# A two-layer MoE kernel behind memory attention: the second matrix of layer two by seven block products

## The chip, the cores and the metric

The kernel runs on one core of one Trainium2 chip. The metric is the device time of one execution in microseconds. TensorE multiplies matrices and writes PSUM; VectorE and ScalarE do the elementwise work; SyncE (SP) issues nearly all DMAs. GpSimd does almost nothing here.

## The reference

Four batches of 576 tokens go through attention over 32 memory slots a head; its output, as 2304 rows of 512, goes through two MoE layers, each of two matrices with an activation between. All inputs are 8-byte floats that the kernel itself decodes to 4-byte ones.

```
h = x @ w_in                      # 2304 x 512 by 512 x 2048
g = np.maximum(0.01 * h, h)       # layer one
return g @ w_out                  # 2304 x 2048 by 2048 x 512

h = x @ w_in                      # layer two, same sizes
sp = np.where(h > 20.0, h, np.log1p(np.exp(np.minimum(h, 20.0))))
g = h * np.tanh(sp)               # Mish
return (g @ w_out).astype(np.float32)
```

## The kernel before

**Precision.** Every operand of the large matmuls is split into a high part (rounded to float32r) and a low part (the rest), and a product is made of three passes: high by high, high by low, low by high. `hi_lo` (line 308) makes the two parts: a copy on ScalarE or VectorE and a difference on VectorE.

**Layer one** (`stage1`, line 888) works on 128 items, one for a batch, a half of its tokens (288) and 128 of the 2048 inner columns. An item has 6 matmuls of 288 columns on line 899 and 12 on line 932; ScalarE and VectorE make the activation's high and low part between them.

**Layer two** works on super-tiles of 768 tokens (three of them) and units of 256 inner columns (eight a super-tile, 24 units in all). `unit` (line 1243) makes the first matrix by Strassen's scheme in Winograd's form: the 2 x 2 blocks of activations and weights are combined into seven products instead of eight, each of 6 matmuls of 384 columns (line 1262). Its sums of results lie in PSUM (banks `h0`, `h1`) and in SBUF; `keep` (line 1292) copies a running sum out on ScalarE before the next product is added to it, `plus` (line 1295) adds on VectorE, and `mish` (line 1275) applies the activation twice, once into the high part and once in full, from which VectorE takes the low part.

The second matrix, `second` (line 1324), is a plain one: a unit has four blocks (two of inner columns, two of tokens), each with three token tiles by three passes, 36 matmuls of 512 columns a unit (line 1336). They accumulate over the eight units of a super-tile in six PSUM banks; then the six are copied out and written, one DMA or more for each (line 1396). Its weights are split once, in `split_w_out` (line 1143), and stay in SBUF for all three super-tiles.

**Weights of layer two** are loaded, decoded and put to DRAM while layer one runs (the loop at line 851, 16 pairs, paced by `W2` and `W2S`). The combined parts of the first matrix are made in the first eight units (`split_w`, line 1080), saved to DRAM, and loaded back in later units.

**Order.** Nothing is written in its final order by hand. Every piece of work is a task with engines, a planned duration, a priority in units of items, the tasks it depends on and the buffers it takes. `Order.run` (line 94) plays the tasks through once and writes each engine's instructions in the order in which it places them. The engines then run their queues in that order, each waiting at its head. SP's queue has loads, saves and outputs in one line.

```
            {"ACT": act(n, ps), "DVE": dve(n) if ps else dve2(n)}, prio, lambda e: copy(e, hi(), src()), deps, take, use,
            lambda e: nc.vector.tensor_tensor(out=lo(), in0=src(), in1=hi().bitcast(F32), op=ALU.subtract),
                    out=ac[t].t, lhsT=(lb if x else hb).t[:, t * P:(t + 1) * P], rhs=wu[0].t[:, wi, :],
```

## Time and profile before

| what | value |
|---|---|
| median of 3 runs | 789.77 us (789.52 to 789.93) |
| profiled execution | 786.6 us |
| its span, first to last instruction | 784.8 us |
| TensorE busy | 767.2 us, 98% |
| VectorE busy | 449.1 us, 57% |
| ScalarE busy | 366.7 us, 47% |
| DMA | 133.27 MB, mean 170 GB/s |
| mean granted clock of TensorE | 0.995 |

Layer one lies roughly between 41 and 405 us, layer two between 393 and 777. Sums and comparisons are made against the profiled execution, since durations come from it; the median of the runs is 3.2 us above it. Busy time of TensorE is modelled at the end of a matmul and counts overlaps, so the distance from one start to the next is the measure of what a matmul costs.

### The profile page before, as it was taken

What the parts mean: (1) busy time and instruction counts of PE and PEld (TensorE: products, weight loads), DVE (VectorE), ACT (ScalarE), POOL (GpSimd) and SP (SyncE); (2) the same over time, 40 slices, a digit from 0 to 9 for tenths busy, and PEclk for the clock granted to TensorE, in tenths of its full rate; (3) what the DMA queues carried; (4) which work ended last, traced back from release to release, by engine and by line L of the source; (5) the groups of instructions that cost most, each with busy time, mean ns of one, the idle gap of its engine ahead of it and who ended that gap; (6) DMA issues with size and microseconds to landing.
All of it is one profiled execution on the core that took longest, in us unless ns stands there. A gap on an engine that the chain in (4) does not pass through costs nothing.

```text
span 784.8 us, 13670 instructions
## 1 busy us (share of the span) xinstructions
PE 767.2 (98%) x5328; PEld 694.7 (89%) x5328; DVE 449.1 (57%) x945; ACT 366.7 (47%) x829; POOL 0.7 (0%) x6
## 2 busy tenths in 40 slices
PE   7999999999999999999999999999999999999996
PEld 5798899998889989999998898888988898889884
DVE  3899868969666875674765566452223272122212
ACT  2576548655454664543554343334332344233322
POOL 0000000000000000000000000000000000000000
PEclk9999999999999999999999999999999999999998
DMA  9995496927978567531744444335432346334303
GB/s 221 266 335 150 133 262 190 299 70 228 300 225 262 165 215 268 162 109 54 280 177 162 174 175 161 121 120 175 134 121 94 122 134 188 108 115 136 98 1 80
DMA packets 57728, 133.27 MB, mean 170 GB/s; under 512 B 5184, under 2 KB 31808, under 8 KB 57664
## 3 DMA queue, kind: packets, MB, share of 16 engines
q1 hardware_dynamic: 57504, 132.14, 54.2%
q8 instruction: 42, 0.69, 0.4%
q10 hardware_dynamic: 160, 0.26, 0.2%
q14 instruction: 22, 0.18, 0.1%
HBM read 100.40 MB, written 31.98 MB: 169 GB/s over the span
## 4 chain that ended last, share of the span: by engine, by line
PE 87%; DMA 5%; DVE 4%; ACT 2%; issue 1%; SPq 0%; ACTq 0%; DVEq 0%
PE h_t L1262 22%; PE acc_t L932 22%; PE acc_t L1336 17%; PE h_t L899 11%; PE misc_t L1336 9%; DMA raw_t<-in_moe_w_in_dram 2%; DMA raw_t<-in_moe_w_out_dram 2%; PE misc_t L738 2%; PE acc_t L819 2%; PE misc_t L533 1%; PE misc_t L621 1%; DVE wo_t L317 1%; PE misc_t L652 1%; DMA phi_t<-in_phi_dram 1%; DVE lo_t L920 0%
## 5 line engine op out<-in xcount | busy, mean ns | idle before, releaser
L932 PE MATMUL acc_t<-hi_t,wo_t 128*128 128x288 f32 x1024 | 162.2, 299 | 0.9 <-ACT hi_t L913 0.3
L932 PEld LDWEIGHTS acc_t<-hi_t,wo_t 128*128 128x128 f32 x1024 | 142.6, 188 | 10.0 <-issue 6.6
L899 PE MATMUL h_t<-at_t,vw_t 128*128 128x288 f32 x768 | 123.8, 297 | 1.6 <-ACT e_t L913 1.5
L899 PEld LDWEIGHTS h_t<-at_t,vw_t 128*128 128x128 f32 x768 | 108.5, 188 | 3.7 <-ACT e_t L913 3.4
L913 ACT ACTIVATE hi_t<-h_t 128x288 fp32r<-128x288 f32 x128 | 52.6, 411 | 102.3 <-PE acc_t L932 90.0
L1297 DVE TENSOR_TENSOR e_t<-e_t,h_t 128x384 f32<-128x384 f32 x48 | 26.6, 554 | 119.0 <-ACT e_t L301 97.1
L932 PE MATMUL acc_t<-lo_t,wo_t 128*128 128x288 f32 x512 | 90.9, 299 | 0.4 <-DVE lo_t L920 0.4
L1262 PE MATMUL h_t<-xt_t,vw_t 128*128 128x384 f32 x432 | 87.4, 337 | 0.0
L920 DVE TENSOR_TENSOR lo_t<-e_t,hi_t 128x288 fp32r<-128x288 f32 x128 | 57.6, 453 | 46.8 <-ACT e_t L913 23.5
L1262 PEld LDWEIGHTS h_t<-xt_t,vw_t 128*128 128x128 f32 x432 | 77.3, 188 | 6.3
L1262 PE MATMUL h_t<-xt_t,wo_t 128*128 128x384 f32 x384 | 82.3, 335 | 0.0
L932 PEld LDWEIGHTS acc_t<-lo_t,wo_t 128*128 128x128 f32 x512 | 74.5, 188 | 8.0 <-issue 6.5
L1336 PE MATMUL acc_t<-wo_t,hi_t 128*128 128x512 f32 x288 | 79.1, 394 | 0.0
L1262 PEld LDWEIGHTS h_t<-xt_t,wo_t 128*128 128x128 f32 x384 | 68.8, 188 | 4.5
L301 ACT ACTIVATE e_t<-h_t 128x384 f32<-128x384 f32 x48 | 23.5, 490 | 98.1 <-PE h_t L1262 98.1
L1336 PEld LDWEIGHTS acc_t<-wo_t,hi_t 128*128 128x128 f32 x288 | 53.5, 188 | 9.7
L913 ACT ACTIVATE e_t<-h_t 128x288 f32<-128x288 f32 x128 | 52.1, 408 | 0.0
L1279 ACT ACTIVATE hi_t<-e_t 128x384 fp32r<-128x384 f32 x48 | 25.2, 526 | 55.9 <-DVE e_t L1297 53.6
L1287 DVE TENSOR_TENSOR lo_t<-e_t,hi_t 128x384 fp32r<-128x384 f32 x48 | 26.8, 558 | 40.0 <-ACT e_t L1282 39.8
L1287 DVE TENSOR_TENSOR lo_t<-x_t,hi_t 128x384 fp32r<-128x384 f32 x48 | 26.7, 557 | 33.5 <-ACT x_t L1282 33.5
L1336 PE MATMUL acc_t<-wo_t,lo_t 128*128 128x512 f32 x144 | 45.3, 394 | 0.0
L365 ACT ACTIVATE raw_t<-raw_t 128x512 f32<-128x512 f32 x46 | 31.5, 685 | 21.3 <-DMA raw_t<-in_moe_w_in_dram 17.1
(187 smaller groups left out, 1031.1 us busy)
## 6 DMA issues: line engine op xcount, KB each, us to landing
vw_t<-wsum SPq DMA_DIRECT2D x32, 512.0 KB, 3.5
raw_t<-in_moe_w_out_dram SPq DMA_DIRECT2D x24, 512.0 KB, 5.8
win_t<-wscr SPq DMA_DIRECT2D x24, 512.0 KB, 4.3
raw_t<-in_moe_w_in_dram SPq DMA_DIRECT2D x22, 512.0 KB, 5.5
wsum<-vw_t SPq DMA_DIRECT2D x16, 512.0 KB, 3.1
wo_t<-wsum SPq DMA_DIRECT2D x16, 512.0 KB, 3.4
kv_t<-in_k_dram SPq DMA_DIRECT2D x8, 576.0 KB, 10.2
kv_t<-in_v_dram SPq DMA_DIRECT2D x8, 576.0 KB, 11.5
```

The lines of the kernel that those rows point to most:

```text
L301: nc.scalar.activation(out=o, in_=i, func=AF.Copy)
L365: nc.scalar.activation(out=hf(), in_=hf(), func=AF.Copy, scale=2.0 ** -112)
L738: nc.tensor.matmul(out=pss[g].t[M * h:M * (h + 1), :], lhsT=vT[b, g][0].t[rows, h // 2, :], rhs=wbs[g].t[rows, h // 2, :], start=True, sto ...
L899: nc.tensor.matmul(out=h.t, lhsT=us[g][0].t[:, wi, j0:j0 + P], rhs=ats[g][0].t[:, ai, cols], start=(n == 0), stop=(n == 3 * NG - 1),)
L913: nc.scalar.activation(out=o, in_=h.t, func=AF.Prelu, alpha=0.01)
L920: lambda e: nc.vector.tensor_tensor(out=lb.make(), in0=eb.t, in1=hb.t.bitcast(F32), op=ALU.subtract),
L932: nc.tensor.matmul(out=ac[kk].t, lhsT=wu[0].t[:, wi, kk * P:(kk + 1) * P], rhs=(hb if src == 0 else lb).t, start=(first and (wi, src) == ( ...
L1262: nc.tensor.matmul(out=h.t, lhsT=w[:, wi, c0:c0 + P], rhs=xp[b, xi].ap()[:, j], start=(first and j == 0 and k3 == 0), stop=(j == 1 and k3 ...
L1279: {"ACT": act(NB2, ps)}, prio, lambda e: nc.scalar.activation(out=hb.make(), in_=src(), func=AF.Mish), deps, [hb], use
L1287: lambda e: nc.vector.tensor_tensor(out=lb.make(), in0=dst(), in1=hb.t.bitcast(F32), op=ALU.subtract),
L1297: {"DVE": dve(NB2)}, prio, lambda e: nc.vector.tensor_tensor(out=x(), in0=x(), in1=h.t, op=ALU.add), deps, (), [h, *use]
L1336: nc.tensor.matmul(out=ac[t].t, lhsT=(lb if x else hb).t[:, t * P:(t + 1) * P], rhs=wu[0].t[:, wi, :], start=(first and (wi, x) == (0, 0)) ...
```

## The change

The second matrix of layer two is also made by seven block products, over groups ("chunks") of four units. `second` and `split_w_out` go; a function `chunk` comes, called after every fourth unit.

- A unit now leaves its four result blocks, after the activation, in SBUF (24 places of 128 x 384, in slots that held layer one's weights, reused as chunks finish).
- `chunk` forms four sums of blocks a unit on VectorE, in place where it can, and for each of seven products and four units a high part (ScalarE or VectorE) and a low part (VectorE). Each product of a unit is three token tiles by three passes, 9 matmuls of 256 columns.
- A product accumulates over its four units in three PSUM banks of one of two sets ("ways"); the second product of a way is added onto the first. After a product its three tiles are copied or added into output rows in SBUF. After the second chunk of a super-tile the rows are written out, in halves of 256 columns.
- The seven combined weight parts of a pair of units are made during layer one, in high and low parts, and saved to DRAM (`t_scr`). `chunk` loads one part, 256 KB, for every product of a unit, into a ring of eight places.
- The loop that prepares the weights is spread further (`W2S` from 2.9 to 3.8) and takes more buffers, among them the tile of k and v of the attention part, widened to 128 partitions.
- Units 1 and 3 put their sums in the banks `acc0` and `acc1`, which the second matrix does not use yet.

```diff
-    A2=30, S2=2.6, V1=2.4, V2=14, W2=56.0, W2S=2.9, O='phi0 phi1 w0 q0 kv0 w1 kv1 w2 q1 w3', HF1=-8.0, HFS=1.0,
+    A2=30, S2=2.6, V1=2.4, V2=14, W2=56.0, W2S=3.8, O='phi0 phi1 w0 q0 kv0 w1 kv1 w2 q1 w3', HF1=-8.0, HFS=1.0,
...
+    DW=280e3, DQ=1.3, DP=1.5, L4=0.5, L4P=1.6, L4S=0.8, L4T=5.0, MA=6, MV="......rvvrrvvrvr",
...
+    kv_again = tags["kv"].new([P, 3, 1024])
+    opened = add({"SP": 0.0}, K["W2"], lambda e: kv_again.make(), (), [kv_again])
...
+    views = [View(j) for j in range(3)]
+    more = Ring(raw.slots + rawm.slots[3:])
+    w2_scr, t_scr = {}, {}
+    OS = ("B11", "B21", "B22", "T1", "T3", "T2", "T4")
     for n in range(NM):
 
         kind, u = "io"[n % 2], n // 2
         p = K['W2'] + K['W2S'] * n
-        bs = [load_raw(p + 2 * j - 6, kind, 2 * u + j) for j in range(2)]
-        wd = raw.new([P, 2, 512])
+        r0, r1, r2 = more.next(3) if n < K["MA"] else views if K["MV"][n] == "v" else raw.slots
+        bs = [load_raw(p + 2 * j - 6, kind, 2 * u + j, 0, r) for j, r in enumerate((r0, r1))]
+        wd = r2.new([P, 2, 512])
...
+        def fsum(e, wd=wd, sb=sb):
+            sb.make()
+            nc.vector.tensor_tensor(
+                out=sb.t[:, 0:2], in0=wd.t[:, :, 256:512], in1=wd.t[:, 0].rearrange("p (a f) -> p a f", a=2), op=ALU.subtract
+            )
+            nc.vector.tensor_tensor(out=sb.t[:, 2], in0=qd(wd, 1, 1), in1=sb.t[:, 0], op=ALU.subtract)
+            nc.vector.tensor_tensor(out=sb.t[:, 3], in0=qd(wd, 1, 0), in1=sb.t[:, 2], op=ALU.subtract)
...
+        def fhi(e, wd=wd, st=st):
+            st.make()
+            copy(e, st.t[:, 0], qd(wd, 0, 0))
+            copy(e, st.t[:, 1:3].rearrange("p a f -> p (a f)"), wd.t[:, 1])
...
+        def flo(e, wd=wd, st=st):
+            for i, x in ((0, qd(wd, 0, 0)), (1, wd.t[:, 1])):
+                y = st.t[:, 0] if i == 0 else st.t[:, 1:3].rearrange("p a f -> p (a f)")
+                nc.vector.tensor_tensor(out=x.bitcast(F32R), in0=x, in1=y.bitcast(F32), op=ALU.subtract)
...
+        def save1(e, u=u, st=st):
+            t_scr[u][0] = dram.tile([P, 7, 2, 256], F32, name=f"tscr{u}")
+            nc.sync.dma_start(out=t_scr[u][0][:, 0:3, 0], in_=st.t[:, 0:3].bitcast(F32))
+
+        def save2(e, u=u, wd=wd):
+            nc.sync.dma_start(out=t_scr[u][0][:, 0, 1], in_=qd(wd, 0, 0))
+            nc.sync.dma_start(out=t_scr[u][0][:, 1:3, 1], in_=wd.t[:, 1].rearrange("p (a f) -> p a f", a=2))
...
+    g_places(2)
     places(1)
-    w_out_place.extend(place([P, 2, 512]) for _ in range(NM - 2))
+    g_places(6)
+    for _ in range(4):
+        b = place([P, 2, 512])[1]
+        T_place.extend(Part(b, lambda t, j=j: t[:, j].rearrange("p (a f) -> p a f", a=2)) for j in range(2))
+    g_places(4)
...
-    def split_w_out(u):
...
+    CH = 4
+    free_g = list(g_place)
+    g_at = {}
+    GN = ("A11", "A12", "A22", "A21")
...
+        s0, s1 = (h_tag.slots[0], h_tag.slots[1]) if n >= CH or n % 2 == 0 else (acc_tag.slots[0], acc_tag.slots[1])
+        ea, e1, e2 = s0.new([P, NB2]), s1.new([P, NB2]), s1.new([P, NB2])
...
-        for q, m, g, (hb, lb, ts) in ((1, 0, 0, c11), (4, 1, 1, c22), (5, 0, 1, c12), (6, 1, 0, c21)):
-            second(n, s, u, i + q * q4 + 0.6 + K["GL"], 2 * u + m, g, hb, lb, ts, u == 0 and m == g, u == NU - 1 and m != g, end and q == 6)
...
+    PROD = (("P1", "A11", "B11", 0), ("P7", "S3", "T3", 1), ("P6", "S2", "T2", 0), ("P4", "A22", "T4", 1), ("P5", "S1", "T1", 0), ("P2", "A12", "B21", 1), ("P3", "S4", "B22", 0))
+    A_WAY = {"P1": (0, 0), "P6": (1, 0), "P5": (1, 1), "P3": (0, 1), "P7": (1, 1), "P4": (1, 0), "P2": (0, 0)}
...
+        for k7, (nm, a, tn, way) in enumerate(PROD):
+            tasks = []
+            for u in range(CH):
+                pa, p = pair[u], at_p(k7, u)
+                p0 = p - K["L4P"]
+                b = {x: pa[x][0] for x in GN}
+                done = {x: pa[x][1] for x in GN}
+                if nm == "P7":
+                    eb = e_tag.new([P, NB2])
+                    ts = sub(
+                        p0 - K["L4S"], lambda eb=eb: eb.make(), b["A11"].ap, b["A21"].ap, ALU.subtract, [done["A11"], done["A21"]],
+                        [eb], [b["A11"], b["A21"]],
+                    )
+                    pa["S3"] = ts
...
+                hb, lb = hi_tag.new([P, NB2], F32R), lo_tag.new([P, NB2], F32R)
+                th = add(
+                    {"ACT": act(NB2), "DVE": dve2(NB2)}, p0, lambda e, hb=hb, src=src: copy(e, hb.make(), src()), dep, [hb], [use],
+                    {"DVE": K["HI"]},
...
+                part = T_place[n_t % 8]
+                tb = part.new()
+                j7 = OS.index(tn)
+                ld = load(
+                    p - K["L4T"], lambda tb=tb: tb.ap().bitcast(F32), lambda u=us[u], j7=j7: t_scr[u][0][:, j7], 262144,
+                    t_scr[us[u]][1] + (T_loads[-1:] if n_t % 2 else []), [tb, *fresh(part)],
...
+            def mms(ts_, hb, lb, tb, u, first_of=first_of, ac=ac):
+                T = tb.ap()
+                for t in ts_:
+                    if u == 0 and first_of:
+                        ac[t].make()
+                    for n3, (x, wi) in enumerate(((hb, 0), (hb, 1), (lb, 0))):
+                        nc.tensor.matmul(
+                            out=ac[t].t, lhsT=x.t[:, t * P:(t + 1) * P], rhs=T[:, wi],
+                            start=(u == 0 and n3 == 0 and first_of), stop=(u == CH - 1 and n3 == 2), skip_group_check=True,
...
+                if fresh_o:
+                    ob = part.new()
+                    got = [ob, *fresh(part)]
+                    dep = [state[g, t, 1 - k2][1]] if c == 0 and nm in ("P6", "P3") else []
+                    ev = add(
+                        {"ACT": act(256, True), "DVE": dve(256)}, pe_p, lambda e, ob=ob, t=t, ac=ac: copy(e, ob.ap(), ac[t].t),
+                        [prev[t], *dep], got, [ac[t]],
                     )
+                else:
+                    ob, pv = state[key]
+                    ev = add(
+                        {"DVE": dve(256)}, pe_p,
+                        lambda e, ob=ob, t=t, ac=ac: nc.vector.tensor_tensor(out=ob.ap(), in0=ob.ap(), in1=ac[t].t, op=ALU.add),
+                        [prev[t], pv], (), [ac[t], ob],
+                    )
+                state[key] = (ob, ev)
+                outs[way][t] = ev
...
+                if half2 and nm in ("P4", "P5", "P2", "P3"):
+
+                    def fo(e, g=g, t=t, k2=k2, ob=ob):
+                        x = (2 * s + g) * NB2 + t * P
+                        end = x + P
+                        while x < end:
+                            b, cc = divmod(x, S)
+                            n3, p0 = divmod(cc, PR)
+                            r = 2 * (n3 % 3) + n3 // 3
+                            n = min(PR - p0, end - x)
+                            o = x - (end - P)
+                            nc.sync.dma_start(out=out_b[b, r, p0:p0 + n, k2 * 256:(k2 + 1) * 256], in_=ob.ap()[o:o + n, :])
+                            x += n
...
+        if n % CH == CH - 1:
+            chunk(n // CH)
```

Three places show what the program's order becomes. The first is TensorE's queue in the middle of layer two. `h0` and `h1` are the first matrix's sums, `acc` the second's, `wo` and `vw` weights, `hi` and `lo` the parts of the activations. Before:

```order
L1336 MATMUL acc0_t_5627<-wo8_t_5537,hi_t_5835 128x512 x2
L1336 MATMUL acc1_t_5632<-wo8_t_5537,hi_t_5835 128x512 x2
L1336 MATMUL acc2_t_5639<-wo8_t_5537,hi_t_5835 128x512 x2
L1262 MATMUL h0_t_5787<-at_t_5461,vw_t_5252 128x384 x2
L1262 MATMUL h0_t_5787<-at_t_5464,vw_t_5252 128x384
L1262 MATMUL h0_t_5787<-at_t_5461,vw_t_5252 128x384 x2
L1262 MATMUL h0_t_5787<-at_t_5464,vw_t_5252 128x384
L1336 MATMUL acc0_t_5627<-wo8_t_5537,lo_t_5838 128x512
L1336 MATMUL acc1_t_5632<-wo8_t_5537,lo_t_5838 128x512
L1336 MATMUL acc2_t_5639<-wo8_t_5537,lo_t_5838 128x512
```

and now:

```order
L1347 MATMUL h1_t_7405<-xt_t_5383,wo1_t_5553 128x384 x2
L1347 MATMUL h1_t_7405<-xt_t_5413,wo1_t_5553 128x384
L1347 MATMUL h1_t_7405<-xt_t_5383,wo1_t_5553 128x384 x2
L1347 MATMUL h1_t_7405<-xt_t_5413,wo1_t_5553 128x384
L1498 MATMUL acc0_t_6780<-wo13_t_5732,hi_t_7366 128x256 x2
L1498 MATMUL acc0_t_6780<-wo13_t_5732,lo_t_7368 128x256
L1498 MATMUL acc1_t_6786<-wo13_t_5732,hi_t_7366 128x256 x2
L1498 MATMUL acc1_t_6786<-wo13_t_5732,lo_t_7368 128x256
L1498 MATMUL acc2_t_6791<-wo13_t_5732,hi_t_7366 128x256 x2
L1498 MATMUL acc2_t_6791<-wo13_t_5732,lo_t_7368 128x256
L1347 MATMUL h0_t_7382<-xt_t_5381,vw_t_5562 128x384 x2
L1347 MATMUL h0_t_7382<-xt_t_5397,vw_t_5562 128x384
```

A block of the second matrix had its high passes and, after a product of the first matrix, its low passes; now the nine matmuls of one product and unit stand together, tile by tile, between two products of the first matrix.

The second place is TensorE's queue where layer one ends and the first units begin. Before:

```order
L1262 MATMUL h_t<-at_t,vw_t 128x384 x6
L932 MATMUL acc_t<-lo_t,wo_t 128x288 x4
L1262 MATMUL h_t<-xt_t,wo_t 128x384 x2
L1262 MATMUL h_t<-wo_t 128x384
L1262 MATMUL h_t<-xt_t,wo_t 128x384 x2
L1262 MATMUL h_t<-wo_t 128x384
L1336 MATMUL acc_t<-wo_t,hi_t 128x512 x6
L1262 MATMUL h_t<-xt_t,wo_t 128x384 x6
L1336 MATMUL acc_t<-wo_t,lo_t 128x512 x3
```

and now:

```order
L1026 MATMUL acc_t<-lo_t,wo_t 128x288 x4
L1347 MATMUL h_t<-xt_t,vw_t 128x384 x12
L1347 MATMUL acc_t<-xt_t,wo_t 128x384 x6
L1347 MATMUL h_t<-at_t,vw_t 128x384 x6
L1347 MATMUL h_t<-xt_t,wo_t 128x384 x2
L1347 MATMUL h_t<-wo_t 128x384
L1347 MATMUL h_t<-xt_t,wo_t 128x384 x2
L1347 MATMUL h_t<-wo_t 128x384
L1347 MATMUL acc_t<-xt_t,wo_t 128x384 x6
L1347 MATMUL acc_t<-xt_t,vw_t 128x384 x6
L1347 MATMUL h_t<-xt_t,wo_t 128x384 x12
```

Units 0 to 3 have products of the first matrix alone; those of two units alternate, one unit's sums in `h`, the other's in `acc`.

The third place is SP's queue near the end: `tscr` are the weight parts in DRAM, `out_0_dram` the output, `x10` and `x11` rows of the output. Before, the last entries are:

```order
L306 DMA vw_t_5386<-wsum72_6340 128x1024
L306 DMA wo2_t_5205<-wsum73_6364 128x2x256
L1396 DMA out_0_dram<-x14_t_8508 96x512
L1396 DMA out_0_dram<-x14_t_8508 32x512
L1396 DMA out_0_dram<-x15_t_8511 64x512 x2
L1396 DMA out_0_dram<-ob_t_8514 32x512
```

and now, some way before the end:

```order
L310 DMA wo11_t_5713<-tscr6_4887 128x512
L1549 DMA out_0_dram<-x10_t_6086 96x256
L1549 DMA out_0_dram<-x10_t_6086 32x256
L310 DMA wo11_t_5713<-tscr7_5213 128x512
L1549 DMA out_0_dram<-x11_t_6200 64x256 x2
L1549 DMA out_0_dram<-x11_t_6200 32x256
L1549 DMA out_0_dram<-x11_t_6200 96x256
L310 DMA wo12_t_5728<-tscr4_4346 128x512
```

Loads of weight parts and writes of output rows now share the queue to the end; at most four writes stand between two loads.

## Rows read from the trace of the kernel before

**Rows 1.** The page's busy line, and its group of weight loads on line 932.

```profile
PE 767.2 (98%) x5328; PEld 694.7 (89%) x5328; DVE 449.1 (57%) x945; ACT 366.7 (47%) x829; POOL 0.7 (0%) x6
...
L932 PEld LDWEIGHTS acc_t<-hi_t,wo_t 128*128 128x128 f32 x1024 | 142.6, 188 | 10.0 <-issue 6.6
```

**Rows 2.** Waits of TensorE: line, what for; us in total, times, longest.

```profile
PE acc_t L465 <- DVE rm_t L451: 1.8, 1, 1.8
...
PE h_t L1262 <- ACT e_t L301: 1.2, 2, 0.6
```

**Rows 3.** Stretches: us, busy of PE, PEld, DVE, ACT, POOL; clock, DMA share, GB/s.

```profile
200.00:320.00 120.00, 119.17 (x1047) 109.94 (x1046) 84.12 (x188) 63.07 (x152) 0.00 (x0) 1.00 0.76 235
405.00:771.00 366.00, 364.84 (x1810) 326.76 (x1810) 146.91 (x268) 140.72 (x293) 0.00 (x0) 1.00 0.40 130
```

**Rows 4.** The same view of the matmuls of line 1336 alone.

```profile
0.00:785.00 785.00, 223.37 (x864) 160.35 (x864) 1.00 0.55 170
```

**Rows 5.** Timeline of TensorE in layer two: start, length, instruction, number merged.

```profile
604.40 1.56 PE L1336 MATMUL acc_t<-wo_t,hi_t 128*128 128x512 f32 x6
605.80 1.20 PE L1262 MATMUL h_t<-xt_t,vw_t 128*128 128x384 f32 x6
606.84 0.86 PE L1336 MATMUL acc_t<-wo_t,lo_t 128*128 128x512 f32 x3
```

**Rows 6.** Timeline of TensorE in layer one; 56 matmuls between the two starts.

```profile
349.76 1.23 PE L932 MATMUL acc_t<-hi_t,wo_t 128*128 128x288 f32 x8
...
357.21 0.96 PE L899 MATMUL h_t<-at_t,vw_t 128*128 128x288 f32 x6
```

**Rows 7.** Timeline of TensorE just before layer one.

```profile
38.33 2.42 PE L819 MATMUL acc_t<-ident 128*128 128x128 f32 x20
40.51 0.38 PE L899 MATMUL h_t<-at_t,vw_t 128*128 128x288 f32 x1
```

**Rows 8.** Timeline of VectorE in layer two, instructions back to back.

```profile
486.81 0.55 DVE L1297 TENSOR_TENSOR x_t<-x_t,h_t 128x384 f32<-128x384 f32 x1
487.27 0.42 DVE L317 TENSOR_TENSOR wo_t<-raw_t,wo_t 128x256 fp32r<-128x256 f32 x1
487.61 1.82 DVE L1216 TENSOR_TENSOR raw_t<-x_t 128x768 f32<-128x768 f32 x2
```

**Rows 9.** Groups from 405 us on: busy us, mean ns of one, idle before.

```profile
L1287 DVE TENSOR_TENSOR lo_t<-x_t,hi_t 128x384 fp32r<-128x384 f32 x48 | 26.7, 557 | 33.5 <-ACT x_t L1282 33.5
...
L1106 DVE TENSOR_TENSOR raw_t<-raw_t 128x256 f32<-128x256 f32 x10 | 4.2, 420 | 0.8 <-DMA raw_t<-w2scri 0.8
...
L1279 ACT ACTIVATE hi_t<-e_t 128x384 fp32r<-128x384 f32 x46 | 24.2, 526 | 54.8 <-DVE e_t L1297 52.5 <-PE acc_t L1336 2.0
```

**Rows 10.** Timeline of TensorE at the first change of super-tile.

```profile
528.20 1.21 PE L1262 MATMUL h_t<-xt_t,vw_t 128*128 128x384 f32 x6
529.98 1.31 PE L1262 MATMUL h_t<-at_t,vw_t 128*128 128x384 f32 x6 [0.58 <-ACT e_t L301]
```

**Rows 11.** Timeline of the end: the last matmuls, and SP's issues.

```profile
776.41 0.63 PE L1336 MATMUL acc_t<-wo_t,lo_t 128*128 128x512 f32 x2
...
775.60 2.06 SPq L1396 DMA_DIRECT2D out_dram<-x_t  x4
777.75 1.25 SPq L1396 DMA_DIRECT2D out_dram<-ob_t  x2
779.09 2.55 SPq L1396 DMA_DIRECT2D out_dram<-x_t  x4
```

**Rows 12.** DMA issues: what, queue, number, size each, median us to landing.

```profile
wo_t<-wsum SPq DMA_DIRECT2D x16, 256.0 KB, 3.2
```

313 lines of the change are left out of this document (178 added, 135 removed).

## Prediction

> **What bounds the kernel now.** I read the page's busy line first, then the waits of the TensorE queue, then the stretches, then single starts in the timeline. The busy line has TensorE at 767.2 us of the 784.8 us span [rows 1]. Busy time alone proves little, because ends of matmuls are modelled; the waits decide. In the whole of layer two TensorE waits for ScalarE twice, 1.2 us together [rows 2], and in the stretch from 405 to 771 us it is busy 364.84 of 366 us while VectorE has 146.91 and ScalarE 140.72 [rows 3]. So layer two is as long as its matmuls, and what a change of their number and width does is read from the spacing of their starts. DMA has room there: share 0.40 [rows 3].
>
> **Spacings.** Six matmuls of 512 columns take 1.40 us from the first start to the next group's, 0.2333 each; six of 384 columns take 1.04, 0.1733 each [rows 5]. Of 288 columns, 56 start between 349.76 and 357.21: 0.1330 each [rows 6]. Of 128 columns (plain f32, the warming ones), 20 take 2.18 us: 0.109 each [rows 7].
>
> **The removed work.** The old second matrix is 864 matmuls of 512 columns, and all of them stand on one line [rows 4]: 864 x 0.2333 = 201.6 us.
>
> **The added matmuls.** Seven products a unit, three token tiles, three passes: 63 a unit of 256 columns, 24 units, 1512. No matmul of 256 columns with full weights stands in the trace. From 288 to 384 columns the spacing grows by 0.0403 for 96 columns; 32 columns under 288 that gives 0.1196, so 0.120 and 181.4 us. Bounds from the rows: it cannot be dearer than 288 columns, 0.133, 201.1 us; the slope from 384 to 512 carried down gives 0.113, 170.9 us; the line between the 128 and 288 rows gives 0.128, 193.5 us. I take 0.120, since the two nearest rows lie on one line with constant overhead, and the 0.109 of 128 columns shows that a weight load does not need more than that. This term is **-20.2 us** (ends -30.7 and -0.5).
>
> The added matmuls each bring a weight load: 1512 for 864, 648 more. The Trainium skill, Perfetto Trace Analysis, section Identifying the Most-Contended Engine, says that headroom on TensorE is judged by the busy share of the weight loads and not by matmul busy time. By that rule the loads, at 694.7 us of 784.8 [rows 1], are nearly full already: 694.7 / 5328 = 0.130 a load, 1512 x 0.130 = 196.6 us, and with the small terms below 1.1 us of gain is left. The trace speaks against taking it literally: a load counts 188 ns [rows 1] where starts are 133 ns apart [rows 6], so most of a load's count is waiting, and 20 loads with their matmuls pass in 2.18 us [rows 7].
>
> **The added vector and scalar work.** Per unit, four second activations (which made the high parts) go and seven copies come, low parts grow from four to seven, four sums of blocks are new, and 21 evictions of 256 columns come per four units. On VectorE that is 3 + 4 instructions of 384 columns and 5.25 of 256. By durations, 0.557 and 0.420 [rows 9]: 6.1 us a unit, 146 us in all; by starts, 0.46 and 0.34 [rows 8]: 5.0 and 120 us. On top of 146.91, without counting off the old splits, 267 to 293 us of some 350: VectorE stays under TensorE. This costs nothing while matmuls of two units stand side by side, which the order shows from unit 4 to 23: first-matrix products of 1.04 us between chunk products of 9 x 0.120 = 1.08 us, so with three buffers a high and a low part have two such pairs, 4.2 us. Two places lack that cover.
>
> First, units 0 to 3, which now have no second-matrix work beside them. Before, at the two places where a product that needs ScalarE's copy follows its predecessor directly, TensorE idles 0.58 us [rows 10]. In the new order the first four units alternate between two sets of PSUM banks, with a product of the other unit (1.04 us) in between. I take **+0.5 us**; ends 0 and 7 (three such copies in four units at 0.58).
>
> Second, the end. After unit 23 the last chunk runs alone: 87 groups of three matmuls, 261 x 0.120 = 31.3 us. Behind the last sum of unit 23 VectorE's order holds 26 low parts, 9 sums, 22 evictions: 35 x 0.46 + 22 x 0.34 = 23.6 us by starts, 28.7 by durations. It fits, but in bursts: with three buffers for high and low parts, a product's copy and difference (0.526 + 0.557) must pass while two products run (2.16 us), which leaves 1.07; three evictions and a sum in front on VectorE's queue take 1.5, so 0.4 is lost at each of six product changes. **+3 us**; ends 0 and 11 (28 x 0.4).
>
> The heavier super-tile changes at units 8 and 16 take some 11 us more on VectorE, with two units of 14.7 us to spread: **+0.5 us**, ends 0 and 5.
>
> **The loads of weight parts.** 168 loads of 256 KB, 44 MB, are new; layer two moved 130 GB/s x 366 us = 47.6 MB [rows 3]. Together 92 MB in some 350 us, 262 GB/s, a share of 0.8 in proportion; from 200 to 320 us the kernel already lives with 235 GB/s at 0.76 and TensorE 119.17 of 120 busy [rows 3]. A load of 256 KB lands 3.2 us after its issue [rows 12]. Eight slots lead by seven products: 7.6 us in the last chunk, twice that before. On SP's queue, a load waits behind rows of the output, at about 0.6 us each (ten issues in 5.86 us [rows 11]); the order has at most four between two loads, 2.4 us. Cost 0; ends 0 and 7.
>
> **The early part.** Preparing weight parts adds, for each of eight pairs, six VectorE instructions; at 0.34 for 256 columns and 0.12 per further 128 [rows 8] 3.2 us, 26 us in all, some 14 on ScalarE, and 10.5 MB more of writes, over 61 items of layer one. VectorE is busy 84.12 of 120 us there [rows 3]. Each part is several queue entries, none long. **+1 us**; ends 0 and 3 (8 x 0.7 x 0.58: each pair finds VectorE busy and pushes a low part by one instruction).
>
> **The last microseconds.** Before, the last matmuls end at 777.04 and the span 7.8 us later, since ten output issues, in blocks to 781.64, queue on SP [rows 11]. Now the last product's three tiles finish 0.36 us apart, and six issues of half the bytes follow, the six of the product before having had 4.3 us: last issue 3.5 us after TensorE instead of 4.6. **-1.1 us**; ends -2 and +1.
>
> **Sum.** -20.2 + 0.5 + 3 + 0.5 + 0 + 1 - 1.1 = -16.3 us. It is made against the profiled execution, 786.6 us (span 784.8): 770.3. The runs shown have a median of 789.77, 3.2 us above the profiled one; carried over, **773.5 us**.
>
> **Rivals.**
> *Slower: weight loads set the pace.* If a stream of 256 columns (107 ns, by 0.42 ns a column from rows 5 and 6) no longer hides its load, spacing stays where 288 columns are, 0.133. For it: nothing under 0.13 with float32r weights stands in the trace, and the loads are busy 89%. Against: 0.109 at 128 columns [rows 7]. Gain 0.5, other terms +3.9: 793.2 us. It decides above 0.131 (201.6 - 3.9 over 1512). Halfway, 0.128, it gives -8.1 + 3.9: 785.6.
> The Trainium skill goes further, on the page TensorE: Matmul & The Clock Gate, section Packing small matmuls: a load overlaps running matmuls only when its row group differs. All groups here are full height, so by that rule load and stream would add, 0.109 + 0.107, and the new matmuls alone would take 326.6 us, 918.7 in all. The 384-column rows [rows 5] are 0.173 apart and not 0.269, so it gets under 0.01, inside the slower rival.
> *VectorE paces the last chunk and the super-tile changes.* Upper ends of those two terms in part: +8 over the forecast, 781.5. For it: bursts as above. Against: 75% by starts.
> *Weight parts come late.* One revolution of the ring late by 2 us, 3.5 revolutions in the last chunk: +7, 780.5. Against: 7.6 us of lead.
> *Cheaper than thought.* 0.113: 763.0.
> That the products are not made as said is excluded by the order.
>
> **Chances.** Forecast 0.56 (its own range 768.5 to 778), VectorE 0.17, late parts 0.06, halfway 0.05, cheaper 0.05, slower rival 0.11, of which 0.04 falls within 0.2% (1.6 us, about what a measurement here can tell from no change). Faster 0.89, same 0.04, slower 0.07. The range 768.0 to 786.0 leaves out the cheaper case and the slower rival, 0.16.
>
> **What would show it.** In the changed profile: 1512 matmuls of 256 columns, starts 0.120 apart in unbroken groups; layer two busy on TensorE to 99% outside the last 31 us; VectorE near 0.8 in layer two with idle time ended by ScalarE; waits of TensorE for low parts, some tenths each, in the last chunk; a DMA share near 0.8. A spacing of 0.128 or more would overturn the first term; TensorE waiting for weight parts or for evictions in the middle of layer two would overturn the cover; gaps in layer one beyond a few us would overturn the early part.

## The result, and the profile after

The changed kernel takes 770.14 us (767.27 to 770.47, 4 runs) where the kernel before takes 789.64 (789.34 to 789.93, 4 runs): ratio 0.9745, 95% interval 0.9721 to 0.9769. The forecast was 773.5, in a range of 768.0 to 786.0. The profiled execution is the one of 770.12, span 768.3.

The busy line of its page, and the group of the new matmuls (busy us, mean ns of one, idle before):

```profile
PE 751.5 (98%) x5976; PEld 717.8 (93%) x5976; DVE 574.7 (75%) x1225; ACT 418.2 (54%) x934; POOL 0.7 (0%) x6
...
L1498 PE MATMUL acc_t<-wo_t,hi_t 128*128 128x256 f32 x720 | 135.6, 282 | 0.0
```

Against [rows 1] TensorE has 648 matmuls more and 15.7 us less; VectorE has gone from 57% to 75%. As before, busy time proves little, and the spacing says what a matmul costs. The timeline of TensorE in layer two:

```profile
604.81 0.40 PE L1498 MATMUL acc_t<-wo_t,hi_t 128*128 128x256 f32 x2
605.05 0.29 PE L1498 MATMUL acc_t<-wo_t,lo_t 128*128 128x256 f32 x1
...
605.89 1.22 PE L1347 MATMUL h_t<-xt_t,vw_t 128*128 128x384 f32 x6
```

Nine matmuls of 256 columns start between 604.81 and 605.89: 0.120 us each, the value forecast. Over all pairs of 256-column matmuls that follow each other the mean is 0.1200, where 512 columns had 0.2324.

The stretches (us; busy of PE, PEld, DVE, ACT, POOL; clock, DMA share, GB/s):

```profile
200.00:320.00 120.00, 120.00 (x1055) 111.00 (x1054) 95.01 (x206) 66.20 (x158) 0.00 (x0) 1.00 0.77 251
...
405.00:440.00 35.00, 35.00 (x214) 34.95 (x213) 26.43 (x58) 24.58 (x54) 0.00 (x0) 1.00 0.92 332
440.00:480.00 40.00, 40.00 (x280) 40.00 (x279) 37.23 (x76) 25.71 (x56) 0.00 (x0) 1.00 0.91 323
480.00:525.00 45.00, 43.29 (x299) 42.67 (x299) 31.68 (x62) 21.16 (x43) 0.00 (x0) 1.00 0.75 240
525.00:731.00 206.00, 206.00 (x1453) 206.00 (x1452) 134.82 (x275) 100.91 (x210) 0.00 (x0) 1.00 0.78 247
731.00:763.00 32.00, 31.80 (x263) 31.39 (x261) 26.08 (x60) 14.24 (x28) 0.00 (x0) 1.00 0.73 218
```

Read beside [rows 3]: layer two is still as long as its matmuls. Units 0 to 3 (405 to 440) and the last chunk (731 to 763) have no gap to speak of, 525 to 731 has none at all, and 1.7 us are lost between 480 and 525, around the first change of super-tile. The waits of TensorE after 400 us (what for; us in total, times, longest) are these two, where [rows 2] has two of 0.6:

```profile
PE h_t L1347 <- ACT wo_t L305: 1.1, 1, 1.1
PE h_t L1347 <- ACT vw_t L305: 0.6, 1, 0.6
```

The end, in the place of [rows 11]: the last matmuls, and the output issues on SP.

```profile
762.52 0.28 PE L1498 MATMUL acc_t<-wo_t,lo_t 128*128 128x256 f32 x1
...
761.22 1.00 SPq L1549 DMA_DIRECT2D out_dram<-x_t  x2
762.58 1.99 SPq L1549 DMA_DIRECT2D out_dram<-ob_t  x4
764.66 1.00 SPq L1549 DMA_DIRECT2D out_dram<-x_t  x2
```

**Where the time came from, between the two profiles (784.8 to 768.3, 16.5 less).**

| stretch, by starts of matmuls | before | after | difference |
|---|---|---|---|
| start to first matmul of layer one | 40.51 | 43.49 | +3.0 |
| from there to layer one's last matmul | 364.01 | 360.83 | -3.2 |
| from there to the last matmul of all | 372.13 | 358.20 | -13.9 |
| from there to the end of the span | 8.15 | 5.78 | -2.4 |

The second row is no gain: the kernel before had already run 36 first-matrix matmuls of layer two when layer one's last matmul started, the changed one has run 18. The other 18, at 0.174, are 3.1 us that moved into the third row. So layer one is unchanged between these two profiles, and layer two's own gain is 17.1 us. The 3.0 us at the start are most likely scatter of single executions: in the seven profiles here and below with the changed kernel's early part as it is, layer one starts between 41.85 and 43.49 us, and in the one other profile with the old early part it starts at 43.14.

### The profile page after: what moved, and what is told of

The parts are those of the page before. It is cut to its first block, busy times and chain, and to the rows that moved or that the text cites. A ratio compares the mean times of both kernels' runs of the same rounds, so it can differ in the third digit from the quotient of the medians.

```text
span 768.3 us, 16060 instructions
## 1 busy us (share of the span) xinstructions
PE 751.5 (98%) x5976; PEld 717.8 (93%) x5976; DVE 574.7 (75%) x1225; ACT 418.2 (54%) x934; POOL 0.7 (0%) x6
## 4 chain that ended last, share of the span: by engine, by line
PE 89%; DVE 4%; DMA 3%; ACT 1%; issue 1%; SPq 0%; DVEq 0%; ACTq 0%
PE acc_t L1026 24%; PE h_t L1347 21%; PE acc_t L1498 17%; PE h_t L993 12%; PE misc_t L1498 7%; DMA raw_t<-in_moe_w_in_dram 2%; PE acc_t L1347 2%; PE acc_t L823 2%; PE misc_t L742 2%; PE misc_t L537 1%; DMA raw_t<-in_moe_w_out_dram 1%; PE misc_t L625 1%; DVE wo_t L321 1%; PE misc_t L656 1%; DMA phi_t<-in_phi_dram 1%
## 5 line engine op out<-in xcount | busy, mean ns | idle before, releaser
L1498 PE MATMUL acc_t<-wo_t,hi_t 128*128 128x256 f32 x720 | 135.6, 282 | 0.0
L1498 PEld LDWEIGHTS acc_t<-wo_t,hi_t 128*128 128x128 f32 x720 | 118.1, 188 | 0.2 <-DVE ob_t L307 0.2
L1498 PE MATMUL acc_t<-wo_t,lo_t 128*128 128x256 f32 x360 | 102.1, 284 | 0.0
L1467 DVE TENSOR_TENSOR lo_t<-wo_t,hi_t 128x384 fp32r<-128x384 f32 x94 | 52.1, 555 | 33.8 <-ACT hi_t L305 32.4
L1347 PEld LDWEIGHTS h_t<-xt_t,vw_t 128*128 128x128 f32 x396 | 67.1, 188 | 0.8 <-ACT vw_t L305 0.8
L1498 PEld LDWEIGHTS acc_t<-wo_t,lo_t 128*128 128x128 f32 x360 | 67.5, 188 | 0.0
L305 ACT ACTIVATE hi_t<-wo_t 128x384 fp32r<-128x384 f32 x83 | 43.5, 524 | 41.7 <-PE acc_t L1498 26.6
L1498 PE MATMUL misc_t<-wo_t,hi_t 128*128 128x256 f32 x288 | 54.7, 282 | 0.0
L1467 DVE TENSOR_TENSOR lo_t<-vw_t,hi_t 128x384 fp32r<-128x384 f32 x50 | 27.7, 556 | 29.8 <-ACT hi_t L305 29.4
L1372 ACT ACTIVATE wo_t<-wo_t 128x384 f32<-128x384 f32 x53 | 27.6, 521 | 34.2 <-DVE wo_t L1366 34.0
```

The costliest lines, as they stand in the source:

```text
L305: nc.scalar.activation(out=o, in_=i, func=AF.Copy)
L1347: nc.tensor.matmul(out=h.t, lhsT=w[:, wi, c0:c0 + P], rhs=xp[b, xi].ap()[:, j], start=(first and j == 0 and k3 == 0), stop=(j == 1 and k3 ...
L1372: lambda e: nc.scalar.activation(out=t_of[x](), in_=h.t if h else t_of[x](), func=AF.Mish),
L1467: lambda e, hb=hb, lb=lb, src=src: nc.vector.tensor_tensor(out=lb.make(), in0=src(), in1=hb.t.bitcast(F32), op=ALU.subtract),
L1498: nc.tensor.matmul(out=ac[t].t, lhsT=x.t[:, t * P:(t + 1) * P], rhs=T[:, wi], start=(u == 0 and n3 == 0 and first_of), stop=(u == CH - 1 a ...
```

## The experiments

Times are beside the kernel before on the same chip, whose median was 789.5 to 790.7 in all of them. Four of the edits make the program place its tasks anew, so that TensorE's order is another one in part of layer two: from 427 us of the changed kernel's profile on with four slots, from 407 with one set of banks, from 418 with two buffers, from 488 with the three edits, each time up to 571. In the last chunk the order is the same in all of them.

**The changed kernel once more.** No edit.

> The changed kernel once more, unaltered, so that the others have a time of the same chip beside them. By my theory the gain is the 1512 matmuls of 256 columns at 0.120 us for 864 of 512 at 0.2324, 19.4 us, and of the small terms little is left: most executions at 770.2 us, some near 767.3, those in which TensorE's clock does not fall before layer one starts. A median of 769 to 771. By the rival that the 767.3 was chance of another kind, no execution comes near it and the profile's first layer-one matmul starts at 43.5 us whatever the time.

Measured: 768.82 us (768.43 to 771.37, 5 runs), ratio 0.975 (0.9732 to 0.9769). In its profile (768.43) layer one starts at 41.85 us instead of 43.49 and its last matmul starts 718.96 us later, against 719.03 in the first profile. In this pair everything behind the start repeats within 0.1 us, and the start scatters. The expectation was right on that place and too simple on the sizes: no execution comes at 770.2 or 767.3, and four of the five lie between 768.4 and 769.3. The later profiles are less even: layer one, which their edits leave alone, takes 360.2 to 362.7 us there from its first to its last matmul, for 360.8 here.

**Four slots for the weight parts.**

```diff
-                part = T_place[n_t % 8]
+                part = T_place[n_t % 4]
```

> The weight parts go round four slots instead of eight. Theory: the loads are hidden only by their lead. With four slots a load can start when the part four products before it is done with, so in the last chunk, where products are 1.08 us apart, it has 3.2 us for an issue of 0.5 and a landing of 3.7: four parts per 5.3 us instead of 4.3, a loss of 0.25 us for each of 28 products, 7 us; in the middle, where first-matrix products stand between, the lead is 6.4 us and nothing is lost. 775 to 780 us. Rival (the loads have slack of another kind, or the last chunk waits for something else anyway): 770 to 771.

Measured: 781.73 us (779.6 to 783.71). From the last first-matrix matmul to the last of all it takes 38.2 us where the changed kernel takes 31.6, so 6.6 lost in the last chunk, as expected; the time is 1.7 us over the expected range. Two of its waits:

```profile
PE h_t L1347 <- ACT wo_t L305: 4.4, 2, 3.8
PE acc_t L1498 <- DMA wo_t<-tscr: 3.9, 3, 2.2
```

The waits for parts (`tscr`) are all in the last chunk; the page puts 0.6 us more there down to a copy on ScalarE, and the rest lies in steps too short for it to name. The middle loses nothing (206.00 busy of 206 from 525 on). So the lead of more than four slots is what keeps the last chunk's loads free; from 525 us to the last chunk four slots would do. Another 5.6 us are lost between 440 and 480, which was not expected:

```profile
440.00:480.00 40.00, 34.37 (x221) 32.91 (x221) 30.29 (x62) 18.55 (x40) 0.00 (x0) 0.96 0.77 258
```

Both waits for ScalarE lie there. After the longer one, 3.8 us to 464.1, the granted clock is at 1.2 GHz from 465.5 to 468.9, and twelve matmuls of 384 columns take 2.9 us instead of 2.1. The order of products there is another one with four slots, so that part can't be put down to late loads.

**One set of PSUM banks for units 0 to 3.**

```diff
-        s0, s1 = (...) if n >= CH or n % 2 == 0 else (acc_tag.slots[0], acc_tag.slots[1])
+        s0, s1 = (...) if True else (acc_tag.slots[0], acc_tag.slots[1])
```

> Units 0 to 3 use the two PSUM banks that the later units use, and no longer alternate with a second set. Theory: the alternation is what hides ScalarE's copies there, since no second-matrix product stands between two first-matrix products in these units; without it up to three copies a unit at 0.58 us are waited for, 2 to 7 us: 772 to 777 us, all of it between 405 and 440 us. Rival: VectorE and ScalarE keep up anyway and the order finds other work: 770 to 771 us.

Measured: 771.71 us (770.59 to 774.71). The stretch from 405 to 440 us:

```profile
405.00:440.00 35.00, 33.28 (x200) 31.93 (x200) 28.66 (x64) 21.68 (x47) 0.00 (x0) 1.00 0.95 359
```

and TensorE's waits there:

```profile
PE h_t L1347 <- ACT wo_t L305: 1.6, 3, 0.6
```

1.7 us are lost there, in three waits for ScalarE's copies of up to 0.6 us; with the alternation none. The mechanism was right, and the price just under the expected 2 to 7, since only three of the copies are waited for in four units. Since the order differs too, these three waits are what the run shows, and not that each microsecond of its longer time is theirs (layer two as a whole is 2.2 us longer).

**Two buffers for high and low parts.**

```diff
+    hi_c, lo_c = Ring(hi_tag.slots[:2]), Ring(lo_tag.slots[:2])
...
-                hb, lb = hi_tag.new([P, NB2], F32R), lo_tag.new([P, NB2], F32R)
+                hb, lb = hi_c.new([P, NB2], F32R), lo_c.new([P, NB2], F32R)
```

> High and low parts of the second-matrix products go round two buffers instead of three (layer one keeps three). Theory: the loss of 3 us that was forecast for the last chunk is not there because the third buffer gives a whole product more of lead, and VectorE's bursts fit in it. With two, copy and difference (0.53 + 0.56 us, and two handovers) must pass while one product of 1.08 us runs: 0.3 to 0.5 us lost on each of 28 products of the last chunk, 8 to 14 us, and nothing in the middle, where a first-matrix product of 1.04 us stands between: 778 to 785 us. Rival (there is so much slack on ScalarE and VectorE in the last chunk that bursts never mattered): under 2 us, 770 to 772.

Measured: 773.54 us (772.09 to 774.62). The last chunk takes 34.5 us for 31.6: 2.9 lost, 0.1 a product and not 0.3 to 0.5. The third buffer matters, and less than the theory says. By the starts, 1.6 us are lost ahead of matmuls with low parts, at 9 places, and 1.8 us ahead of high parts, at some 20; half of the 1.8 is the single step right behind a late low part, 0.1 us longer each time. The median is 4.7 us over the changed kernel's on this chip; in the profile layer two is 3.1 us longer, and layer one, which is not what the edit is about, 2.2. Copy and difference need not both be done when a product begins: the low part is needed only by its third matmul, 0.24 us after the first. That this is the whole reason is argued, not shown.

**The kernel before, its second-matrix matmuls cut in two.**

```diff
-                nc.tensor.matmul(out=ac[t].t, lhsT=..., rhs=wu[0].t[:, wi, :], ...)
+                for c2 in range(2):
+                    nc.tensor.matmul(out=ac[t].t[:, 256 * c2:256 * c2 + 256], lhsT=...,
+                                     rhs=wu[0].t[:, wi, 256 * c2:256 * c2 + 256], ...)
```

> The kernel before, with each of its 864 second-matrix matmuls of 512 columns split into two of 256 (same sums, same copies, same loads of data; each half loads the weights again). It measures the price of the narrower form without Strassen's scheme. Theory: the spacing of 256 columns is 0.120 us whatever stands around, 1728 x 0.120 = 207.4 us for 864 x 0.2324 = 200.8: 6.6 us slower, 796 us. Rival: the doubled number of weight loads sets a pace of its own when they come in this number (0.133): 1728 x 0.133 = 229.8, 29 us slower, 819 us; or the halves cost nothing extra (0.1162 each): 790 us.

This kernel does not compute the reference's sums, and why is open; number, size and order of the matmuls are as said. Measured: 793.31 us (791.71 to 795.55), ratio 1.005 (1.0031 to 1.0069). Twelve matmuls of 256 columns in its timeline:

```profile
604.92 0.64 PE L1337 MATMUL acc_t<-wo_t,hi_t 128*128 128x256 f32 x4
605.41 1.12 PE L1337 MATMUL misc_t<-wo_t,hi_t 128*128 128x256 f32 x8
606.37 1.20 PE L1262 MATMUL h_t<-xt_t,wo_t 128*128 128x384 f32 x6
```

The mean spacing over the whole is 0.1195 us, and layer two, from its first to its last matmul, takes 389.4 us where before it takes 383.7: 5.7 more, as 1728 x 0.1195 = 206.5 for 200.8 demands. So the price of 256 columns is the same without the scheme, and the change's matmul term splits into 5.7 us for the narrower form and -25 us for the 216 matmuls that the scheme saves of 1728.

**128 columns.**

```diff
-                            out=ac[t].t, lhsT=..., rhs=T[:, wi],
+                            out=ac[t].t[:, u % 2 * P:u % 2 * P + P], lhsT=..., rhs=T[:, wi, u % 2 * P:u % 2 * P + P],
```

> The changed kernel with 128 columns instead of 256 in each of the 1512 second-matrix matmuls (units take the left and the right half of the columns in turn, so half of the second matrix is left out); all copies, differences, sums and loads stay. It asks where the weight load would begin to set the pace. Theory of a floor: a matmul cannot follow faster than its weight load, 0.109 us as the plain f32 ones of 128 columns: 1512 x (0.120 - 0.109) = 17 us less TensorE time, 752 to 756 us, and spacings of 0.109. Rival (the columns alone set the spacing, 13 ns and 0.417 a column as at 256, 288 and 384): 0.067 us, TensorE time down by 80 us; then DMA and VectorE bind and the time is 700 to 730 us.

Measured: 759.58 us (759.3 to 759.85), some 4 us over the expected 752 to 756. The timeline in an unbroken group:

```profile
602.66 0.39 PE L1498 MATMUL acc_t<-wo_t,hi_t 128*128 128x128 f32 x2
602.88 0.27 PE L1498 MATMUL acc_t<-wo_t,lo_t 128*128 128x128 f32 x1
602.99 0.39 PE L1498 MATMUL acc_t<-wo_t,hi_t 128*128 128x128 f32 x2
603.21 0.28 PE L1498 MATMUL acc_t<-wo_t,lo_t 128*128 128x128 f32 x1
```

The next matmul starts at 603.33, so these are six starts in 0.67 us, 0.111 each, and weight loads start at the same distance: half the columns make a matmul 9 ns cheaper. The floor is there, and at 256 columns the kernel runs 9 ns above it. What happens at the edges of a group fits a floor that the loads set:

```profile
605.47 0.34 PE L1498 MATMUL acc_t<-wo_t,hi_t 128*128 128x128 f32 x2
605.64 0.28 PE L1498 MATMUL acc_t<-wo_t,lo_t 128*128 128x128 f32 x1
...
606.42 1.28 PE L1347 MATMUL h_t<-xt_t,wo_t 128*128 128x384 f32 x6
607.53 0.34 PE L1498 MATMUL acc_t<-wo_t,hi_t 128*128 128x128 f32 x2
```

Behind matmuls of 384 columns, whose 0.174 leaves time for the next loads, the second matmul of a group follows the first after only 0.060 us (at all 126 such places), which is near the rival's 0.067; every later one takes some 0.11. And the six of 384 columns behind a group take 1.11 us instead of 1.04, their first step 0.228. Layer two is 11 us shorter: the steps from and to 384 columns counted in, a matmul costs 0.113 where it cost 0.120.

**Low parts twice.**

```diff
+            for _ in range(2):
+                nc.vector.tensor_tensor(out=lb.t, in0=src(), in1=hb.t.bitcast(F32), op=ALU.subtract)
```

> Each of the 168 low parts of layer two's second matrix is computed twice (the second writes the same numbers again): VectorE gets 168 x 0.46 = 77 us more. Theory: VectorE has real slack in the middle (135 busy of 206 us) and none to speak of in the last chunk (26.1 of 32, and 28 x 0.46 = 12.9 more) or where the first chunk runs beside the sums for the next super-tile (440 to 480 us: 37.5 of 40): 7 us lost in the last chunk, 5 to 8 in 440 to 525, nothing between 525 and 731: 780 to 787 us. Rival (busy time of VectorE overstates by so much that bursts still fit): under 3 us, up to 772. Rival of the other side (VectorE's queue paces TensorE in every unit): 800 and more.

Measured: 802.09 us (801.4 to 803.77), 33 us over the changed kernel and well over the expectation; only the rival of the other side has such a time. Its stretches:

```profile
480.00:525.00 45.00, 39.29 (x251) 37.91 (x252) 38.56 (x74) 20.18 (x42) 0.00 (x0) 0.96 0.71 225
525.00:731.00 206.00, 199.28 (x1386) 197.96 (x1385) 178.53 (x363) 93.70 (x199) 0.00 (x0) 0.99 0.78 251
```

And its two longest waits of TensorE after 400 us:

```profile
PE h_t L1347 <- DVE wo_t L1366: 9.2, 6, 2.7
PE acc_t L1503 <- DVE lo_t L1417: 4.8, 13, 0.7
```

Between 525 and 731, where nothing was to be lost, TensorE idles 6.7 us at 178.5 of VectorE's 206 (0.87); the last chunk, from the last first-matrix matmul to the last of all, takes 41.2 us for 31.6. By the starts, ahead of the last chunk 21 us are lost in front of first-matrix products, for the sums of line 1366, which they need at once (11.4 us by the page), and for ScalarE's copies (4.8), and under 1 us in front of low parts; in the last chunk, which has no first-matrix product, 7.5 of 9.9 us are lost in front of low parts. So VectorE's queue does not pace TensorE in every unit, as that rival has it: added work in it is paid by whatever short step stands behind it. Part of the cost is the clock: behind two of the waits, of 2.7 and 3.1 us, it is at 1.2 GHz, from 498.0 to 501.4 and from 539.0 to 542.4 us.

**More warming matmuls.** 19 more of them, at the two idle places before layer one.

```diff
-        nc.tensor.matmul(out=warm..., lhsT=ident, rhs=ident, start=True, stop=True)
+        n_spin[0] += 1
+        for _ in range(1 + {10: 9, 13: 10}.get(n_spin[0], 0)):
+            nc.tensor.matmul(out=warm..., lhsT=ident, rhs=ident, start=True, stop=True)
```

> The changed kernel with 19 more warming matmuls, whose results nobody reads, at the two places before layer one where TensorE idles 1.4 and 1.7 us (at 19.5 and 23.0 us of the profile) and after which its granted clock is at the lower level for some 10 us. Theory: the idle time is what lets the clock fall; with TensorE busy there it stays at the upper level, the first matmul of layer one comes at 40 to 41 us instead of 41.9 to 43.5, and all executions are at 766.5 to 768 us. Rival: the start is set by loads and by VectorE (1.9 of 2 us busy there), the clock is only a witness, and the added matmuls come on top: 769 to 773 us, with layer one starting at 42 to 45 us.

Measured: 770.78 us (769.33 to 772.32); in the profile layer one starts at 46.1 us, later even than the rival's 42 to 45. The theory fell: TensorE stood still all the same, for 2.6 us, earlier in its work and after the same number of matmuls, give or take one. The profiled execution is the slowest of the four, with a mean granted clock of 0.994. The other three have 0.998 to 0.999, so the clock hardly fell in them, and still take 769.3 to 770.9 us and not the theory's 766.5 to 768.

**Fewer warming matmuls, and two more edits.** Both leave out the warming steps 8 to 19; the second also has these two.

```diff
-        p = n1 - K["XL"] if s == 0 else pr(s * NU) - 4.0
+        p = n1 - K["XL"] if s == 0 else pr(s * NU) - 5.5
...
-                            nc.sync.dma_start(out=out_b[...], in_=...)
+                            (nc.scalar if to_act else nc.sync).dma_start(out=out_b[...], in_=...)
```

> The changed kernel without twelve of its warming steps (24 matmuls by the profile, results nobody reads), those on either side of the place before layer one at which TensorE stood still for 1.0 to 4.0 us in every profile so far, always after its 220th or 221st matmul, which is its 449th instruction, with no wait that the profile shows, and always starting again between 23.1 and 25.3 us; in the run with more warming it stood there too, at the same instruction, and so that run's theory (idle time for want of work) fell. Theory now: the stop belongs to that place in the instruction stream, it ends at about the same time whatever TensorE did before, and what then delays layer one is what still has to be done after it, warming at the lower clock included. With 2.8 us of warming less behind it, layer one starts 2 to 3 us earlier, at 39 to 41 us, and the time is 766 to 768 us. Rival: VectorE and the loads set the start of layer one whatever TensorE does: 769 to 770.5 us, start at 41.9 to 43.5. Rival of the other side: without this work the clock stays low for longer: over 771 us.

> The same with two more edits, to see the two other places at which TensorE or the end wait in the changed kernel. The input parts of the second and third super-tile are made 1.5 units of the plan earlier: theory, the waits of 1.1 and 0.6 us for ScalarE at unit 8 (480 to 525 us) go, -1.3 us or more of the 1.7 us lost there; rival, they only move to another place on ScalarE's or VectorE's queue, 0. And two of the last six output issues go to ScalarE's queue: theory, the time from TensorE's last matmul to the end is set by six issues in a row on SP, and is 4.2 us instead of 5.5; rival, the last issue is bound by the last eviction, 5.2 to 5.5. Together 2.6 us below the run with fewer warming steps by the theories, 0 to 0.3 by the rivals.

Measured: 768.39 us (767.95 to 770.35) and 767.86 (765.68 to 768.11), ratios 0.9736 (0.9719 to 0.9752) and 0.9718 (0.9701 to 0.9735). Fewer warming: layer one starts at 42.05 us, inside the rival's 41.9 to 43.5, and the time lies between the theory's range and the rival's; the stop of unknown cause is gone, and in its place, and to about the same time, TensorE waits for a load:

```profile
PE acc_t L537 <- DMA kv_t<-in_v_dram: 2.9, 1, 2.9
```

The earlier input parts: the waits shrink from 1.7 to 1.2 us, but layer two's length is the same within 0.1 us, so the rival holds. The two issues on ScalarE's queue: from the start of the last matmul to the end 4.7 us for 5.9 with fewer warming steps alone, 1.2 of the 1.3 expected. The three together have the lowest median of the runs that compute everything. They beat the kernel before by far; against the changed kernel's two medians, 770.14 and 768.82, they are 1 to 2 us lower, but the intervals of the ratios overlap, so that they are faster than the changed kernel is not shown by the times.

**Twenty more warming steps at the very beginning.**

```diff
+        for _ in range(1 + {1: 20}.get(n_spin[0], 0)):
```

> The changed kernel with twenty more warming steps (40 matmuls by the profile, results nobody reads) at its very beginning, where TensorE waits for the first loads anyway. It asks what the stop before layer one, which the profile puts down to nothing, hangs on. If it belongs to the place in the instruction stream, TensorE now stands still after its 220th matmul again, which is no longer the first warming one after the scores' first product but lies inside or just behind the 48 matmuls of line 537 near 17 to 19 us, and goes on between 20 and 25 us; the place where it stood before is then passed without a stop of its own. If it belongs to the work (a hidden wait of that warming matmul), the stop stays where it was, after the 260th. The time says nothing here: 768 to 773 us by either.

Measured: 772.61 us (772.33 to 772.9). The timeline of TensorE:

```profile
17.04 1.29 PE L537 MATMUL acc_t<-kv_t,phi_t 96*32 96x128 f32 x37
22.30 1.07 PE L537 MATMUL acc_t<-kv_t,phi_t 96*32 96x128 f32 x11 [3.98 <-issue]
```

and in the DMA view the instruction queue between 19 and 21 us (packets, MB, share of 16 engines):

```profile
q8 instruction: 1, 0.02, 3.8%
```

The stop now cuts a run of equal matmuls of one tile in two, after the 221st, and the place where it stood before is passed without one: it belongs to the place in the instruction stream.

## Why the prediction was right, and where its sizes were off

The bound, the mechanism and the side were right; the time is 3.4 us under the forecast, and the terms show why.

- **Matmuls, -20.2.** Measured by mean spacings: 1512 x 0.1200 = 181.4 for 864 x 0.2324 = 200.8, -19.4. The carried-down line through 288 and 384 columns gave the 0.120 exactly; the 0.8 is in the 512 columns, whose six starts in [rows 5] gave 0.2333. The steps around the new matmuls give back some of the 19.4 (see the remainder, below).
- **Units 0 to 3, +0.5.** Measured 0: the alternation covers all, and costs 1.7 when it is gone.
- **Last chunk, +3.** The mis-sized term: by the starts 0.26 us lost, at one place (732.7 us), and none of the forecast waits for low parts. (0.4 us at each of six changes is also 2.4 us and not 3.) VectorE's total was right (26.1 us for 23.6 by starts and 28.7 by durations), but the working put three evictions and a sum in front of one low part. The order spreads them. Its VectorE at the one change of the six with three evictions in a row; at the other five a low part stands behind the first of the three:

```profile
740.73 0.55 DVE L1467 TENSOR_TENSOR lo_t<-vw_t,hi_t 128x384 fp32r<-128x384 f32 x1
741.20 0.41 DVE L1533 TENSOR_TENSOR x_t<-x_t,acc_t 128x256 f32<-128x256 f32 x1
741.53 0.74 DVE L1533 TENSOR_TENSOR x_t<-x_t,misc_t 128x256 f32<-128x256 f32 x2
742.19 0.55 DVE L1467 TENSOR_TENSOR lo_t<-wo_t,hi_t 128x384 fp32r<-128x384 f32 x1
742.66 0.55 DVE L1422 TENSOR_TENSOR vw_t<-vw_t 128x384 f32<-128x384 f32 x1
```

  The sums stand behind a low part and not in front of it, and evictions alone (0.99 us here) fit the 1.07 that was worked out. The runs with two buffers and with doubled low parts show that the bound as such is real. In all of layer two VectorE is busy 256 of 358 us by the rows above (405 to 763), 0.72, a little under the forecast's 0.8.
- **Changes of super-tile, +0.5.** 1.7 us of waits by the page for 1.2 before (2.3 for 1.7 by the starts): right in size, all of it at or soon after the first change and none at the second.
- **Weight parts, 0.** Right, and in the last chunk for the reason given: with half the slots 6.6 us are lost there, and none in the middle.
- **Early part, +1.** Measured 0 between the two profiles: layer one's length is the same within 0.1 us, with VectorE at 95.0 of 120 us for 84.1 [rows 3].
- **Last microseconds, -1.1.** Measured -2.4, beyond even that term's end of -2: the issues before the last six had left SP free at 762.22, so the last six start 0.06 us after the last matmul's start and are through 2.9 us after the last matmul's end, where 3.5 was forecast; from there to the end of the span it is 2.7 us for 3.2 before.
- **The step to the median.** The sum without the start, -19.5 (-17.1 and -2.4), is what the medians on this chip show (789.64 to 770.14); on the chip of the second run they show -21.0 (789.85 to 768.82). Carrying the 3.2 us over to the median came out right, without a reason given at the time. Most likely the profiled execution of before had an early start: in the run with its matmuls cut in two, whose part ahead of layer two is the same, layer one starts at 43.14 us for 40.51. Its other executions have no profile.
- **The remainder.** -19.4 + 0.3 in the last chunk + 0.5 of more waits is -18.6, and layer two's own gain is 17.1. The sum over all its starts, by the matmul before each, places the rest. Steps behind second-matrix matmuls go from 200.5 to 182.5 us, steps behind first-matrix ones from 177.8 to 178.7. Without waits, the step from a group of 256 columns to 384 takes 0.124 and not 0.120 (0.5 us in all), and steps behind 384 columns have a mean of 0.1758 for 0.1747 (1.1 us in all), nearly all of it between the fifth and the sixth of a group, 0.185 for 0.175. It repeats in the second profile, and is not there in the kernel before with its matmuls cut in two (0.1735); why that step is longer, no run shows.

So the matmuls of layer two brought 17.9 us where 20.2 were forecast, and its small terms cost 0.8 where 4 were forecast. The two errors have opposite signs: that layer two came within 0.9 us of its forecast is in part luck.

Of the rivals, the weight loads came nearest to the truth. They do set a pace, 0.111 us, and 256 columns pass 9 ns above it. The Trainium skill, Perfetto Trace Analysis, section Identifying the Most-Contended Engine, would judge TensorE's headroom by the arithmetic done against the peak (MFU) and by the busy share of the loads. That share rose from 89% to 93%, and 648 more loads went in while TensorE's time fell. A load's record is 188 to 191 ns long whether it is followed after 0.174, 0.120 or 0.111 us, so here the share does not tell how far the floor is; the spacings of a narrower form do. (Against the floor of 0.111, 77 of the 188 ns are not needed: less than the "most" that the prediction takes.)

## What to carry to other kernels

Where TensorE is the bound and its queue unbroken, price an edit by starts, form by form; a straight line through the two nearest widths gave the third to the nanosecond, until the loads' own pace, which one run with narrower matmuls finds. Work moved to an engine that is 75% busy is free only through buffers and slots that lead far enough: halve each of them once, and you see which of them carries the change. And before a profiled span is compared with another, take off the start: a stretch that the change does not touch can hold as much as the terms that are argued about. What is then still missing can be found by summing every step, sorted by the matmul before it: here most of it was in steps of a form that the change had left alone.
